# One core, one fixed set of instructions, another written-out order: new costs and priorities in a planner for linear attention and a gated MLP

## The chip, the cores and the metric

The kernel runs on one core of a Trainium2 chip. The metric is the device time of one launch in microseconds (us). The median of three runs of the kernel before is 784.33 us; they lie between 782.07 and 785.16 us.

## What is computed

The reference is linear attention with softmax-like features, followed by a block that gates, normalises and projects. Cut to what matters:

```python
def phi(x):                                   # q, k: 8 batches, 8 heads, 576 rows, 64 wide
    proj = einsum('bhsd,df->bhsf', x, w_phi)  # 128 features
    proj = proj - max(abs(proj), axis=-1)
    return concatenate([exp(proj), exp(-proj)], axis=-1)
kv, z = einsum('bhsf,bhsd->bhfd', phi(k), v), sum(phi(k), axis=2)
x = einsum('bhsf,bhfd->bhsd', phi(q), kv) / (einsum('bhsf,bhf->bhs', phi(q), z) + 1e-6)
x = x.transpose(0, 2, 1, 3).reshape(4608, 512)
h = x @ w_in                                  # 512 -> 1024
solu = h * exp(h - max(h)) / (sum(exp(h - max(h))) + 1e-9)
out = (layer_norm(solu) * g_ln) @ w_out       # 1024 -> 512
```

## The kernel before

**The attention half** works in 16 units of four heads (unit u is half of the heads of batch u // 2), and each unit in two halves of two heads ("sub" 0 and 1). For the keys, five tiles of rows are loaded (`rawk`), split into a rounded part and a rest (`xh`, `xl`; not in the first three units), projected on TensorE (`pjk`), reduced and shifted on VectorE (`m`, `dk`) and exponentiated on ScalarE (`ek`). `visit` (L651) then does all the small matmuls of a half: the sums over rows (`kvT`) and, from the seventh half on, in one stretch with it the numerators and denominators of the half before (`num`, `den`). The result is turned on VectorE (`kvs`), written to DRAM (`dk`) and read back in four pieces (`kvf`, L719).

For the queries, each half from unit 3 on loads one block of 128 x 1152 numbers, 576 KB, the "q rows" (`q_load`, L783, tile `rawq`). ScalarE rounds it (`q_hi`, L787, a cast to `hq`), GpSimd forms the rest in place (`q_lo`, L791), TensorE projects (`pq`), VectorE turns it and takes a maximum, and after a small chain over TensorE, GpSimd and ScalarE the features `fq` are made on ScalarE. The denominators go through VectorE (`den_recip`, L893: `dE`, `cmp`, `cmr`), to DRAM (`den_rows`, L903) and come back copied to 64 partitions each (`den_bcast`, L907, tile `rb`, two transfers per half). GpSimd multiplies (`xa`, `xb`).

**The second half** works on 36 tiles of 128 tokens. For each: split of x (`mxh`, `mxl`), 24 matmuls for h, maximum on VectorE (`moe_max`, L1149, `nm`), exponential on ScalarE (`moe_exp`, L1153, `eu`), product on VectorE (`eu` again), statistics (`bst`, `mv`), eight transposes (`uT`), a split into `uh` (ScalarE) and `ul` (VectorE), 24 matmuls for the output (`o`), scaling on ScalarE (`os`) and a store.

**The order.** Work of both halves is interleaved, and no scheduler runs on the chip: each engine executes its instructions in the program's order (L345 hands each instruction on with the order kept, which is why the profile shows that one line for nearly all). The order is worked out once, while the program is built, by `Plan.order` (L212). It is a list planner: each operation has an engine, a cost in nanoseconds, predecessors and tiles. At each step each engine looks at the operations that could go next. The one that could start first on it by the plan's clock is taken (TensorE may wait a little to keep its array's tiling); the priority, BASE[group] + OFFSET[kind] (L197), decides only among those that could start at that same moment. Groups are the 16 units, the 36 token tiles and the weights (53 numbers), kinds the operations within them (688 numbers). Buffers are handed out in the order of the priorities too.

A transfer has two costs, the time that it holds the issuing queue (SP, the only queue used) and the time on the DMA engines. Its landing, and what follows from it, are planned so:

```python
hold, transfer = o["cost"]
engine_free[e] = t + hold
dma_free = done[i] = max(t + hold + 625, dma_free) + transfer   # L301
# a successor may start 910 after done (1150 on TensorE), L163
```

The costs that the change touches are `dma()` at L139 for plain blocks, and figures of their own for the four pieces of `kvf` (L1019), the q rows (L1042), and the broadcasts `rb` (L1109). `den_recip` has its cost at L1105. The exponential's cost and predecessor are at L1234, the cast's at L1043.

Of the kernel before, what the change touches and what calls it, by code (L numbers as in the profile page):

```python
# [22 lines left out]
HC = S // 2  # L23
# [36 lines left out]


BASE = (
# [4 lines left out]
)  # L67
OFFSET = (
# [47 lines left out]
)  # L116


# [4 lines left out]
def dve(n):  # L123
    return (n + 65) / 0.96
# [12 lines left out]


def dma(nbytes, spread=False):  # L139
    return (580 if spread else 440), max(nbytes / 360.0, 50)  # L140


class Plan:
# [213 lines left out]
def linear_attention_then_moe(ctx: ExitStack, tc, qT, qT2, kT, v, w_phi, w_in, g_ln, w_out, out):  # L357
# [181 lines left out]
    for i in range(8):  # L539
        z, R, T = w_time[i], ("raw", i), ("w32", i)  # L540
# [406 lines left out]
    for u in range(2 * B):  # L947
# [6 lines left out]
        def add(name, engine, cost, t, fn, args, after=(), alloc=(), tiles=(), early=None):  # L954
            name = (u, *name)
            q = lambda names: [x[1] if x[0] == "abs" else (u, *x) for x in names]
            op(name, engine, cost, z0 + t * step, fn, (st, *args), q(after),
               [(tag, x[1] if x[0] == "abs" else (u, *x)) for tag, x in alloc], q(tiles), early)

        for g, (c0, n) in enumerate(TILES):  # L960
            nt, n2 = n // P, 2 * n
            z = 2.0 * g
# [28 lines left out]
        for sub in range(2):  # L991
# [23 lines left out]
            if u not in KV_PE:  # L1015
                add(("kve", sub), "vector", dve(384) + 40, z, kv_turn, (sub,), [prev], [("d", ("kvs", sub))], [("kv", sub)])
                add(("kvo", sub), "sync", dma(P * 384 * 4), z, kv_out, (sub,), [("kve", sub)], (), [("kvs", sub)])
                for i in range(4):
                    add(("kvi", sub, i), "sync", (620, 137), z, kv_in, (sub, i),  # L1019
                        [("kvi", sub, i - 1) if i else ("kvo", sub)], () if i else [("kf", ("kf", sub))], [("kf", sub)])  # L1020
            else:
                add(("kve", sub), "scalar", act(384, True), z, kv_ev, (sub,), [prev], [("d", ("kvs", sub))],
# [16 lines left out]
        for sub in range(2):  # L1039
            z = 5.0 * sub + 1.0  # L1040
            if qsp:
                add(("ql", sub), "sync", (400, 1640), z - 4, q_load, (sub,), (), [("q4", ("rq", sub))])  # L1042
                add(("qh", sub), "scalar", act(2 * S), z - 2.5, q_hi, (sub,), [("ql", sub)], [("q4", ("hq", sub))],  # L1043
                    [("rq", sub)])
                add(("qlo", sub), "gpsimd", pool(2 * S) + 130, z - 2.2, q_lo, (sub,), [("qh", sub)], (),
# [56 lines left out]
                add(("qv", sub, c), "scalar", act(HC, True), z + 5.1 + c, q_oe, (sub, c),  # L1102
                    [source["num"]] + ([("qv", sub, 0)] if c else []), () if c else [("E", ("E", sub))],
                    [("num", sub, c), ("E", sub)])
            add(("dc", sub), "vector", dve(HC) + 27 + 330, z + 6.3, den_recip, (sub,), [source["den"]],  # L1105
                [("dE", ("dE", sub))], [("den", sub)])
            add(("ds", sub), "sync", (380, 100), z + 6.5, den_rows, (sub,), [("dc", sub)])
            for j in range(2):
                add(("db", sub, j), "sync", (560, 600), z + 6.9, den_bcast, (sub, j),  # L1109
                    [("ds", sub)] + ([("db", sub, 0)] if j else [("db", 0, 1)] if sub else []), () if j else [("rb", ("rb", sub))],  # L1110
                    [("rb", sub)])
            pair = 2 * qd + sub
# [188 lines left out]
```

## Time and profile before

| | us |
|---|---|
| median of three runs | 784.33 |
| the profiled execution | 785.97 |
| its span, first to last instruction | 783.9 |
| TensorE busy (PE) | 754.0 |
| VectorE busy (DVE) | 500.1 |
| GpSimd busy (POOL) | 471.1 |
| ScalarE busy (ACT) | 384.5 |

The mean granted clock of TensorE over the span is 0.986 of full speed. A table by windows has one row per stretch: its bounds and length, then for each engine the busy time and in brackets the number of instructions, then the granted clock, the busy share of the DMA engines and GB/s. A line of the timeline has the start, the length, engine, instruction, tiles (written <- read), count, and in square brackets the idle time of that engine just before it with what ended it. PE's matmuls are pipelined, so its busy time is a cover of the time axis and not a sum of work; where PE is "busy" at half clock it does half the work.

### The profile page before, as it was taken

The page shows a single profiled execution, that of the slowest core. Times are in us where ns is not written, and L with a number is a line of the kernel's source. Part 1 is how long each engine was busy: PE and PEld are TensorE (multiplying, and loading weights), DVE is VectorE, ACT ScalarE, POOL GpSimd, SP SyncE. Part 2 cuts the span into 40 slices and gives each one's busy share as a digit, 9 for nine tenths or more (in the row PEclk, how much of TensorE's full clock was granted, in tenths as well). Part 3 has the DMA queues.
Part 4 walks back from the last instruction along what each step waited for, and adds up shares of the span by engine and source line. Part 5 has one row for each costly group of instructions (what it writes and reads, how often), then busy time and mean ns, then how long its engine had stood idle before and what let it go on. Part 6 is the DMA issues. An engine that isn't in the chain of part 4 may idle for free.

```text
span 783.9 us, 13479 instructions
## 1 busy us (share of the span) xinstructions
PE 754.0 (96%) x4935; PEld 566.1 (72%) x4935; DVE 500.1 (64%) x861; ACT 384.5 (49%) x750; POOL 471.1 (60%) x507
## 2 busy tenths in 40 slices
PE   5899999999999999989999999999999999999997
PEld 3566677767777777767776777777778776778885
DVE  3897986665775676756777657765457665444343
ACT  3757765363736445544636463633546454223221
POOL 1144788686977658676767786855677775132110
PEclk8899999999999999989999999999999999999999
DMA  7843532243415152433424342414241222110001
GB/s 233 313 148 103 138 88 84 69 144 77 129 50 158 53 141 79 117 89 102 114 57 135 95 148 62 127 56 136 77 129 44 56 56 58 42 43 13 28 15 40
DMA packets 99969, 75.35 MB, mean 96 GB/s; under 512 B 56128, under 2 KB 90432, under 8 KB 99392
## 3 DMA queue, kind: packets, MB, share of 16 engines
q1 hardware_dynamic: 99904, 74.50, 32.6%
q8 instruction: 39, 0.64, 0.3%
q14 instruction: 26, 0.21, 0.1%
HBM read 59.38 MB, written 15.09 MB: 95 GB/s over the span
## 4 chain that ended last, share of the span: by engine, by line
PE 55%; DVE 3%; DMA 2%; SPq 1%; ACT 1%; POOL 1%; issue 0%; ACTq 0%; POOLq 0%
PE o L345 18%; PE h L345 17%; PE kvT L345 5%; PE num L345 5%; PE uT L345 3%; PE pjk L345 2%; PE den L345 2%; PE pq L345 2%; DMA rawq<-in_q 2%; SPq L345 1%; DVE bst L345 0%; DVE eu L345 0%; DMA rb<-d 0%; DVE cmp L345 0%; DVE ul L345 0%
## 5 line engine op out<-in xcount | busy, mean ns | idle before, releaser
L345 ACT ACTIVATE ek<-dk 128x512 f32<-128x512 f32 (+1 forms) x160 | 88.2, 582 | 61.3 <-DVE dk L345 55.7
L345 PE MATMUL o<-w_out_h,uh 128*128 128x512 f32 x288 | 115.7, 402 | 1.2 <-DVE ul L345 1.1
L345 PE MATMUL o<-w_out_l,uh 128*128 128x512 f32 x288 | 114.1, 396 | 0.0
L345 PE MATMUL o<-w_out_h,ul 128*128 128x512 f32 x288 | 114.1, 396 | 0.0
L345 POOL TENSOR_TENSOR zacc<-zacc,ek 128x512 f32<-128x512 f32 (+1 forms) x78 | 100.8, 1292 | 18.6 <-ACT ek L345 15.2
L345 PE MATMUL h<-win_h,mxh 128*128 128x512 f32 x288 | 94.1, 408 | 0.0
L345 PE MATMUL h<-win_l,mxh 128*128 128x512 f32 x288 | 91.3, 398 | 0.0
L345 PE MATMUL h<-win_h,mxl 128*128 128x512 f32 x288 | 91.1, 397 | 0.0
L345 DVE TENSOR_TENSOR ul<-uT,uh 128x512 fp32r<-128x512 f32 x72 | 48.7, 683 | 49.2 <-ACT uh L345 49.0
L345 POOL TENSOR_TENSOR hq<-rawq,hq 64x1152 fp32r<-64x1152 f32 x26 | 69.1, 2659 | 16.6 <-ACT hq L345 14.9
L345 DVE TENSOR_REDUCE nm<-h 128x1 f32<-128x1024 f32 x36 | 44.0, 1222 | 52.6 <-PE h L345 52.5
L345 ACT ACTIVATE fq<-pT 128x576 f32<-128x576 f32 x104 | 68.5, 676 | 16.4 <-PE den L345 6.7
L345 POOL TENSOR_TENSOR blk<-blk,mcol 128x1152 f32<-128x1152 f32 x26 | 55.5, 2135 | 26.2 <-ACT mcol L345 20.6
L345 ACT CAST uh<-uT 128x512 fp32r<-128x512 f32 x72 | 41.5, 583 | 57.6 <-PE uT L345 39.0
L345 PE MATMUL num<-fq,kvf 128*64 128x288 f32 x512 | 69.2, 412 | 0.6 <-DMA kvf<-dk 0.6
L345 ACT ACTIVATE eu<-h,nm 128x1024 f32<-128x1024 f32 x36 | 40.2, 1117 | 59.5 <-DVE nm L345 59.1
L345 DVE TENSOR_TENSOR eu<-h,eu 128x1024 f32<-128x1024 f32 x36 | 44.0, 1223 | 36.5 <-ACT eu L345 36.5
L345 DVE TENSOR_REDUCE m<-pjk 128x4 f32<-128x512 f32 (+1 forms) x80 | 48.7, 623 | 24.9 <-PE pjk L345 24.5
L345 PEld LDWEIGHTS h<-win_l,mxh 128*128 128x128 f32 x288 | 54.7, 190 | 13.3
L345 PEld LDWEIGHTS h<-win_h,mxl 128*128 128x128 f32 x288 | 54.6, 190 | 13.2
L345 PEld LDWEIGHTS o<-w_out_h,uh 128*128 128x128 f32 x288 | 54.2, 188 | 13.8 <-DVE ul L345 1.9
L345 PE MATMUL kvT<-ek,rawv 128*64 128x256 f32 x512 | 64.0, 382 | 0.0
(107 smaller groups left out, 1571.7 us busy)
## 6 DMA issues: line engine op xcount, KB each, us to landing
rawq<-in_q SPq DMA_DIRECT2D x26, 576.0 KB, 5.1
rb<-d SPq DMA_DIRECT2D x64, 144.0 KB, 3.3
out<-os SPq DMA_DIRECT2D x36, 256.0 KB, 2.0
rawk<-in_k SPq DMA_DIRECT2D x64, 128.0 KB, 2.7
rawv<-in_v SPq DMA_DIRECT2D x64, 128.0 KB, 2.3
dk<-kvs SPq DMA_DIRECT2D x28, 192.0 KB, 1.9
kvf<-dk SPq DMA_DIRECT2D x112, 48.0 KB, 2.5
wraw<-in_w_in SPq DMA_DIRECT2D x4, 1024.0 KB, 6.0
```

Of the source, the lines that this page charges most:

```text
L345: return self.tc.keep_in_program_order(method(*args, **kwargs))
```

## The change

No operation is added, removed or resized: the same operations with the same predecessors, tiles and buffers go through the same planner. Changed are five lines of costs and the 741 priorities. A plain transfer is reckoned at 300 instead of 360 bytes per nanosecond; the q rows at 440 + 2600 instead of 400 + 1640 ns; each broadcast at 640 + 950 instead of 560 + 600; each piece of `kvf` at 660 + 160 instead of 620 + 137; `den_recip`'s three VectorE instructions at 880 ns together instead of dve(288) + 357 = 724.7.

```diff
 def dma(nbytes, spread=False):
-    return (580 if spread else 440), max(nbytes / 360.0, 50)
+    return (580 if spread else 440), max(nbytes / 300.0, 50)
...
-                    add(("kvi", sub, i), "sync", (620, 137), z, kv_in, (sub, i),
+                    add(("kvi", sub, i), "sync", (660, 160), z, kv_in, (sub, i),
...
-                add(("ql", sub), "sync", (400, 1640), z - 4, q_load, (sub,), (), [("q4", ("rq", sub))])
+                add(("ql", sub), "sync", (440, 2600), z - 4, q_load, (sub,), (), [("q4", ("rq", sub))])
...
-            add(("dc", sub), "vector", dve(HC) + 27 + 330, z + 6.3, den_recip, (sub,), [source["den"]],
+            add(("dc", sub), "vector", 880, z + 6.3, den_recip, (sub,), [source["den"]],
...
-                add(("db", sub, j), "sync", (560, 600), z + 6.9, den_bcast, (sub, j),
+                add(("db", sub, j), "sync", (640, 950), z + 6.9, den_bcast, (sub, j),
```

The priorities are new numbers near the old ones. The first lines of BASE (weights, then units 0 to 13) as an example:

```diff
-    -335.3, -1579.6, -520.2, 46.7, 148.7, 211.0, 261.8, 299.0, 351.4, 396.6, 438.6, 480.4, 527.0, 577.2, 625.0,
+    -420.3, -1654.0, -538.8, 32.5, 142.5, 205.1, 253.3, 303.4, 345.0, 393.4, 437.9, 482.8, 527.3, 576.3, 639.9,
```

OFFSET changes in the same manner. Counted from 0, its numbers 604 and 605 belong to the load and the cast of the q rows of sub 0 from unit 4 on, 635 and 636 to those of sub 1: they go from -34.3, -33.3, -36.0 and -19.9 to -29.8, -16.8, -36.5 and -15.8.

100 rows, old and new, of tables (BASE, OFFSET) are left out of this document.

## The prediction

> **What bounds the kernel now.** First the page, for the span and the busiest engine:
>
> ```profile
> span 783.9 us, 13479 instructions
> PE 754.0 (96%) x4935; PEld 566.1 (72%) x4935; DVE 500.1 (64%) x861; ACT 384.5 (49%) x750; POOL 471.1 (60%) x507
> ```
>
> TensorE (PE) is busy for 754.0 of 783.9 us. No instruction is removed, so a new order can only win back the remaining 29.9 us and what half clock costs. The table by windows, cut at the places where PE was idle, says where they are:
>
> ```profile
> core 0: us, PE busy (x) PEld busy (x) DVE busy (x) ACT busy (x) POOL busy (x), PEclk, DMA share, GB/s
> 0.00:10.00 10.00, 4.70 (x12) 3.20 (x12) 3.48 (x7) 3.33 (x6) 2.27 (x17) 1.00 0.59 176
> 10.00:20.00 10.00, 5.65 (x12) 3.43 (x13) 4.18 (x9) 3.27 (x6) 0.00 (x0) 0.59 0.94 297
> 20.00:30.00 10.00, 8.50 (x82) 5.53 (x80) 9.34 (x9) 6.80 (x11) 2.36 (x1) 0.90 1.04 410
> 30.00:40.00 10.00, 8.45 (x50) 5.41 (x50) 8.62 (x13) 8.60 (x16) 1.39 (x1) 0.83 0.63 223
> 40.00:110.00 70.00, 65.30 (x624) 45.74 (x616) 61.69 (x91) 46.67 (x104) 43.00 (x28) 1.00 0.42 116
> 110.00:170.00 60.00, 59.53 (x401) 44.35 (x402) 41.06 (x79) 29.61 (x61) 47.04 (x51) 1.00 0.32 97
> 170.00:178.00 8.00, 6.26 (x36) 4.69 (x34) 4.56 (x9) 6.58 (x14) 7.61 (x10) 1.00 0.50 115
> 178.00:285.00 107.00, 106.62 (x705) 80.37 (x706) 69.02 (x128) 50.83 (x99) 74.15 (x76) 1.00 0.35 96
> 285.00:290.00 5.00, 4.18 (x23) 3.44 (x22) 3.72 (x10) 4.86 (x11) 4.51 (x7) 1.00 0.40 111
> ...
> 338.00:342.86 4.86, 2.71 (x35) 1.73 (x27) 3.36 (x6) 3.76 (x7) 4.72 (x3) 1.00 0.04 14
> 342.86:349.69 6.83, 6.11 (x18) 4.98 (x19) 5.10 (x9) 3.72 (x9) 5.82 (x10) 0.50 0.40 87
> 349.69:426.00 76.31, 76.31 (x526) 57.43 (x524) 50.99 (x94) 39.32 (x78) 56.02 (x54) 1.00 0.36 104
> 426.00:434.00 8.00, 6.79 (x38) 5.56 (x37) 7.27 (x15) 5.04 (x11) 7.44 (x11) 1.00 0.50 125
> 434.00:770.00 336.00, 335.92 (x2032) 257.99 (x2031) 193.11 (x332) 144.84 (x276) 179.83 (x211) 1.00 0.24 69
> 770.00:784.00 14.00, 8.98 (x41) 6.64 (x39) 3.07 (x6) 2.44 (x4) 0.75 (x2) 0.97 0.10 37
> ```
>
> From 434 to 770 us PE is idle for 0.08 of 336 us at full clock: nothing to win, much to lose. The last 14 us (5.02 idle) are the drain of the last token tile, a chain that no order shortens much. The first 40 us lose 5.30 + 4.35 + 1.50 + 1.55 = 12.70 us of idle time plus some half clock to first loads and the preparation of weights. Between 40 and 434 us lie 4.70 (40 to 110), 0.47, 1.74, 0.38, 0.82, then 2.15, 0.72 and 1.21 us. Behind the 2.15 the clock was 0.50 for 6.83 us, in which 6.11 busy us did the work of about 3.05. So the two stretches 338 to 350 and 426 to 434 cost 2.15 + 0.72 + 3.05 + 1.21 = **7.1 us**, nearly half of all that the middle can give.
>
> What these two stretches waited for is in the chain of waits. Both times it passes through a transfer of q rows, two of its longest pieces:
>
> ```profile
> 329.08 7.68 DMA rawq<-in_q
> ...
> 413.02 6.07 DMA rawq<-in_q
> ```
>
> The timeline shows how a late transfer reached TensorE. First stretch:
>
> ```profile
> 328.61 0.85 SPq L345 DMA_DIRECT2D rawq<-in_q  x2
> ...
> 333.70 1.23 DVE L345 TENSOR_REDUCE nm<-h 128x1 f32<-128x1024 f32 x1 [1.11 <-PE h L345]
> ...
> 336.84 1.15 ACT L345 CAST hq<-rawq 128x1152 fp32r<-128x1152 f32 x1 [4.89 <-DMA rawq<-in_q]
> ...
> 338.19 1.12 ACT L345 ACTIVATE eu<-h,nm 128x1024 f32<-128x1024 f32 x1
> ...
> 339.43 1.23 DVE L345 TENSOR_TENSOR eu<-h,eu 128x1024 f32<-128x1024 f32 x1 [4.50 <-ACT eu L345]
> ...
> 340.71 0.66 PE L345 MATMUL uT<-ident,eu 128*128 128x128 f32 x4 [1.47 <-DVE eu L345]
> ...
> 343.08 0.58 PE L345 MATMUL pjk<-wph_h,xh 128*128 128x256 f32 x1 [0.91 <-DVE dE L345]
> ...
> 345.23 0.58 PE L345 MATMUL pq<-hq,w_hh 128*128 128x288 f32 x1 [0.49 <-POOL sa L345]
> ```
>
> ScalarE (ACT) keeps program order. It stood 4.89 us before the cast of the q rows, though the exponential `eu` queued behind it had its maximum at 333.70 + 1.23 = 334.93. `eu` ran at 338.19; VectorE waited 4.50 us for it, and behind VectorE's product stood everything that frees TensorE's banks. Second stretch, same shape:
>
> ```profile
> 412.39 1.01 SPq L345 DMA_DIRECT2D rawq<-in_q  x2
> ...
> 416.52 1.22 DVE L345 TENSOR_REDUCE nm<-h 128x1 f32<-128x1024 f32 x1 [0.23 <-PE h L345]
> ...
> 419.17 1.16 ACT L345 CAST hq<-rawq 128x1152 fp32r<-128x1152 f32 x1 [2.22 <-DMA rawq<-in_q]
> ...
> 421.33 1.10 ACT L345 ACTIVATE eu<-h,nm 128x1024 f32<-128x1024 f32 x1
> ...
> 427.79 0.37 PE L345 MATMUL pq<-hq,w_hh 128*128 128x288 f32 x1 [0.60 <-POOL sa L345]
> ...
> 428.90 0.50 PE L345 MATMUL o<-w_out_h,uh 128*128 128x512 f32 x1 [0.60 <-DVE ul L345]
> ```
>
> **The change, part by part.** *The q rows.* Issues and landings (KB each, median us to landing):
>
> ```profile
> rawq<-in_q SPq DMA_DIRECT2D x26, 576.0 KB, 5.1
> rb<-d SPq DMA_DIRECT2D x64, 144.0 KB, 3.3
> ...
> rawk<-in_k SPq DMA_DIRECT2D x64, 128.0 KB, 2.7
> ```
>
> The cast began 0.08 us after the landing (336.84 against 329.08 + 7.68), so a landing of the trace compares with the plan's "usable" time, landing plus 910 ns. For a single block of q rows the plan said 400 + 625 + 1640 + 910 = 3.58 us after the issue; it will say 440 + 625 + 2600 + 910 = 4.58, with 5.1 the median here. For two issued back to back, as at both places, the second was usable 3.58 + 1.64 = 5.22 us after the first issue and will be 4.58 + 2.60 = 7.18. Put on the trace's clock: at 328.61 + 5.22 = 333.83 the old plan saw the cast start before the exponential (maximum at 334.93), so it put the cast first. The new plan has 335.79, after 334.93: exponential first. At the second place it is 417.61 before, the maximum at 416.52 + 1.22 = 417.74, and 419.57 after: the order flips again, and 419.57 is past the real 419.17. The real start at the first place, 336.84, is 1.05 us later than the new figure, so ACT may still stand a little there, but with the exponential done. With the exponential at about 335 instead of 338.19, some 3 us earlier, the 1.47 us wait of `uT` and its followers go, and with them the half clock. Late next is the q chain itself (`hq`, `pq`), whose cast comes no later than now plus one exponential, 1.12 us. Value: **-7.1 us**; bounds 0 (the places come out alike) and -7.1.
>
> On the price of a q row there is a rule that speaks against the change. The Trainium skill, DMA: Bandwidth & Descriptors, Specifications, gives a core some 358 GB/s from memory and 0.6 us to the first byte; worked out from it, an estimate of 2.25 us for 576 KB, the old plan's figure and not the new one's, by which this term would be 0. The median of 5.1 us above disagrees.
>
> *Broadcasts, `kvf`, plain blocks, the reciprocal.* Usable times go from 560 + 625 + 600 + 910 = 2.70 to 3.13 us for `rb` (median 3.3), and from 2.34 to 2.41 for a 128 KB block (440 + 625 + 910 + 131072 / 360 or / 300; median 2.7). Both come nearer to the trace. What waits for `rb` is GpSimd:
>
> ```profile
> POOL xa L345 <- DMA rb<-d: 27.6, 13, 6.5
> SPq L345 <- ACT os L345: 166.7, 26, 14.6
> ```
>
> These 27.6 us are hidden: the page has POOL busy for 60%, and a later `xa` holds up PE only through the token tiles, of which PE has stock (0.08 us idle in the 336 above). Value 0; cover gone, one `rb` wait costs up to 6.5 us. The longer holds (40 ns for each of 8 pieces and 2 q rows, 80 for each of 4 broadcasts, 0.72 us per unit) exist in the plan only; the chip's SP queue stands idle anyway, 166.7 us before stores alone.
>
> *Everything else is dealt anew.* 741 priorities change, so small stalls of other causes vanish and come. None of it is visible in the trace before. The lower bound is that all idle time of 40 to 770 us goes: 4.70 + 0.47 + 1.74 + 0.38 + 0.82 + 2.15 + 0.72 + 1.21 + 0.08 = 12.3, with the half clock 15.3 us. The upper is fresh stalls of the dear kind: 2.15 + 0.72 + 3.05 = 5.9 us each. I take the plain cheap kind, once: the three places at full clock that stand alone are 1.74, 0.82 and 1.21, mean 1.26, so **+1.3 us**, since the old middle has three such in 394 us and priorities near the old ones will keep most of them as they were, so one more is already a third more. The start and the drain I take at 0; PE's first work waits for first loads.
>
> **Sum.** -7.1 + 1.3 = -5.8. The profiled execution took 785.97 us (span 783.9), 1.64 over the median of 784.33. On its own time the sum gives 780.2; on the median **778.5 us**, -0.74%. A difference under 0.5% (3.9 us) can't be told from none here, so "faster" begins below 780.4 and "slower" above 788.3.
>
> **The rivals.**
>
> *Repaid (784.4).* The two stalls go, but the new order makes one cold stall of 5.9 and one plain: -7.1 + 5.9 + 1.3. For it: 394 us of the old middle hold eight idle rows, so stalls come easily. Against: 336 us without any, under the old, shorter costs. The same time follows if the pairs of q rows are ordered as before.
>
> *Slower (789.0): the read-back is late.* Transfers thought longer are issued earlier. SP keeps order: a load put early stands before its buffer is free, and the four pieces of `kvf`, without which a visit's numerators can't start, queue behind it. A visit is at the head of TensorE's queue, so PE stops. It decides when the pieces come over about 2 us late: 1.74 us idle left the clock at 1.00, 2.15 was followed by 0.50. Two such visits cost 11.8: -7.1 + 11.8 = +4.7. For it: SP does wait much (166.7 us before stores). Against: every cost moves towards the measured landing, which makes the plan start consumers later and not loads tighter.
>
> *More than that (772.3).* The two singles 1.74 and 0.82 and half of the 4.70 in 40 to 110 us go as well, with no fresh one: -7.1 - 2.56 - 2.35 = -12.0.
>
> *No clock to win (781.6).* The half clock at 342.86 has a cause other than the idle time before it, and comes back: then the two places give only their idle 4.08, and -4.08 + 1.3 = -2.8. The row speaks against it: the drop follows the 2.15 us at once. The Trainium skill, TensorE: Matmul & The Clock Gate, Why this matters for your kernels, asks for no PE gaps over about 3 us, one idle window bringing half clock; the longest single wait of PE quoted here is 1.47 us, so by that rule the gaps would not have done it. The trace shows several short gaps in one such stretch and the clock at 0.50 behind them.
>
> **How the numbers follow.** Chances: forecast 0.46, more than that 0.13, repaid 0.20, no clock 0.06, slower 0.15. The forecast's own range is 775 to 781.5: no fresh stall and a small one gone, or three fresh ones. About 0.38 of its 0.46 lie below 780.4; with 0.13 and a hundredth of the repaid case that is 0.52 faster. Slower has its 0.15 and 0.02 of the repaid case, 0.17; 0.31 remains for the same. The range 770 to 789 reaches from the lower bound (784.33 - 15.3 = 769.0) with a corner left out to the slower case.
>
> **What would show it.** Right: near the old places, or wherever a pair of q rows is issued, the cast no longer stands more than about 2 us before an exponential that is ready; the granted clock holds 1.00 from 40 us to the drain; PE idle between 110 and 434 us falls from 7.5 us to about 2 to 4; the stretch to 770 stays dense. The landings themselves must stay at 4 to 8 us: if they shrink, the gain came from traffic and not from order. Wrong: a second stretch with clock 0.50 after 40 us; waits of `num` for `kvf` of over 2 us; more idle time before 110 us; or the exponential still queued behind a late cast.

## The result, and the profile after

| | before | after |
|---|---|---|
| median, us | 784.48 (4 runs, 782.07 to 785.16) | 774.28 (4 runs, 772.5 to 775.5) |
| ratio | | 0.9868, 95% interval 0.9842 to 0.9893 |
| profiled execution, us | 785.97 | 773.6 |
| its span, us | 783.9 | 771.7 |
| mean granted clock | 0.986 | 0.993 |

The change is 10.2 us faster, where the prediction had 5.8. The head of the page of the changed kernel:

```profile
span 771.7 us, 13472 instructions
PE 747.6 (97%) x4935; PEld 564.6 (73%) x4935; DVE 498.0 (65%) x861; ACT 384.1 (50%) x750; POOL 471.0 (61%) x507
```

The same 4935 matmuls, with 24.1 us of idle PE instead of 29.9. Where, the table by windows says (columns as in the prediction):

```profile
0.00:40.00 40.00, 27.22 (x156) 16.90 (x156) 27.49 (x39) 22.57 (x39) 7.32 (x20) 0.87 0.78 268
40.00:110.00 70.00, 65.51 (x614) 46.63 (x614) 57.71 (x89) 47.34 (x108) 44.24 (x31) 1.00 0.44 122
110.00:434.00 324.00, 322.38 (x2191) 244.35 (x2190) 220.88 (x408) 169.74 (x334) 245.76 (x252) 1.00 0.37 103
434.00:758.00 324.00, 324.00 (x1942) 250.46 (x1941) 189.29 (x325) 141.98 (x269) 172.94 (x205) 1.00 0.24 68
```

Idle time of the first 40 us is 12.78 us (12.70 before), of 40 to 110 us 4.49 (4.70). From 110 to 434 us it fell from 7.49 to 1.62 us, and the half clock there (3.05 us of work lost) is gone. Those two make 5.87 + 3.05 = 8.9 us. The clock can't be put down to the change, though. A second profile of the kernel before (span 781.5 us, its rows are further down) has the stretch at 1.00, with 7.89 us idle, and the first 40 us at 0.91, where the first profile has 0.83 and the changed kernel 0.87. Against that second profile the change is worth 6.3 us in the stretch, all of it idle time. Of the 9.8 us between those two spans 7.2 us are less idle time of PE (31.3 and 24.1 us); the other 2.6 us lie inside what the page counts as busy (750.2 and 747.6 us), where no view shows them apart.

The casts of the q rows on ScalarE, as the groups of lines have them, first in the kernel before, then in the changed one (count | busy, mean ns | idle before them and what ended it):

```profile
L345 ACT CAST hq<-rawq 128x1152 fp32r<-128x1152 f32 x26 | 30.0, 1154 | 31.8 <-DMA rawq<-in_q 15.4 <-POOL hq L345 12.3 <-DVE pT L345 2.1
```

```profile
L345 ACT CAST hq<-rawq 128x1152 fp32r<-128x1152 f32 x26 | 29.9, 1151 | 11.9 <-POOL hq L345 9.4 <-PE pq L345 1.6 <-DMA rawq<-in_q 0.8
```

ScalarE's standing for q rows went from 15.4 to 0.8 us. The rows also land sooner:

```profile
rawq<-in_q SPq DMA_DIRECT2D x26, 576.0 KB, 4.3
```

4.3 us instead of 5.1. The prediction had said that a gain with shorter landings came from traffic and not from order, so this is a rival. At the two places themselves (sub 0 of units 9 and 11, found by counting loads and casts in the program's order) the difference is larger than in the median:

```profile
317.09 0.54 SPq L345 DMA_DIRECT2D rawq<-in_q  x1
...
322.92 0.33 SPq L345 DMA_DIRECT2D rawq<-in_q  x1
...
325.92 1.12 ACT L345 ACTIVATE eu<-h,nm 128x1024 f32<-128x1024 f32 x1 [1.99 <-PE o L345]
...
327.59 1.15 ACT L345 CAST hq<-rawq 128x1152 fp32r<-128x1152 f32 x1
...
400.28 0.53 SPq L345 DMA_DIRECT2D rawq<-in_q  x1
...
405.93 0.33 SPq L345 DMA_DIRECT2D rawq<-in_q  x1
...
410.67 1.15 ACT L345 CAST hq<-rawq 128x1152 fp32r<-128x1152 f32 x1
```

The two blocks of a unit, issued 0.5 and 0.6 us apart before, are now issued 5.8 and 5.7 us apart. The later one lands 3.8 and 3.5 us after its issue instead of 7.7 and 6.1, and its cast follows an exponential without a wait. From issue to cast it is 4.7 us at both places, where it was 7.8 and 6.2: the use has not moved away from the issue, the rows land faster.

The largest idle place left between 110 and 758 us is another one, a wait of `pq` of the timeline that no transfer ended:

```profile
244.78 0.37 PE L345 MATMUL pq<-hq,w_hh 128*128 128x288 f32 x1 [1.52 <-DVE mt L345]
```

### The profile page after: what moved, and what is told of

Same layout as the page of the kernel before. It is cut to its first block, busy times and chain, and to the rows that moved or that the text cites. A ratio compares the mean times of both kernels' runs of the same rounds, so it can differ in the third digit from the quotient of the medians.

```text
span 771.7 us, 13472 instructions
## 1 busy us (share of the span) xinstructions
PE 747.6 (97%) x4935; PEld 564.6 (73%) x4935; DVE 498.0 (65%) x861; ACT 384.1 (50%) x750; POOL 471.0 (61%) x507
## 4 chain that ended last, share of the span: by engine, by line
PE 93%; DVE 3%; DMA 1%; ACT 1%; SPq 1%; issue 1%; POOL 0%; ACTq 0%; POOLq 0%
PE o L345 26%; PE h L345 26%; PE kvT L345 11%; PE num L345 8%; PE pjk L345 6%; PE uT L345 4%; PE den L345 4%; PE pq L345 4%; DVE w L345 1%; PE pjq L345 1%; PE dT L345 1%; SPq L345 1%; DMA rawk<-in_k 1%; DVE cmp L345 0%; DVE m L345 0%
## 5 line engine op out<-in xcount | busy, mean ns | idle before, releaser
L345 POOL TENSOR_TENSOR blk<-blk,mcol 128x1152 f32<-128x1152 f32 x26 | 55.5, 2135 | 36.5 <-ACT mcol L345 36.3
L345 PEld LDWEIGHTS o<-w_out_h,ul 128*128 128x128 f32 x288 | 54.2, 188 | 13.2
```

The source lines that it names most:

```text
L345: return self.tc.keep_in_program_order(method(*args, **kwargs))
```

## The experiments

Three theories went in. **A**, the prediction's: late q rows at two places, by standing in front of a ready exponential, cost 7.1 us. **B**: all transfers were planned too short, the planner's clock ran too fast everywhere, and places are only where this surfaces. **C**: costs do not matter; the priorities, or the traffic, do. To weigh B a number of the kernel's own is used: the clock on which `Plan.order` lays out the order. Its end is 766.5 us for the order before and 770.0 for the changed one. It can also be added up over a finished order with other costs: the order before, with the new costs, ends at 782.7. These figures are arithmetic of the kernel's code and no measurement; what is measured is how the spans stand to them.

### The two casts behind the exponentials

```diff
-    for o in plan.order():
+    sequence = plan.order()
+    for first, then in (((9, "qh", 0), ("moe", 10, "ex")), ((11, "qh", 0), ("moe", 13, "ex"))):
+        sequence = behind(sequence, first, then)   # `first` and what hangs on it go behind `then`
+    for o in sequence:
```

> The kernel before with its order kept, except at the two places of the prediction: the cast of the q rows (unit 9 and unit 11, sub 0) and the GpSimd subtraction that hangs on it are put behind the exponential that waited behind the cast (token tiles 10 and 13). Theory A (the prediction's: a late block of q rows in front of a ready exponential cost these two places 7.1 us): about 777 us, -7 against before, clock 1.00 from 40 us on, no idle time of TensorE over 0.5 us at either place. Theory B (the places only show where a plan that is too fast everywhere runs out of slack; freed here, the delay comes up at the next place): within 2 us of before. Theory C (the rows land sooner in the changed kernel because they are issued apart): no change, since the issues are as before.

783.85 us against 784.9, ratio 0.9983 (0.9962 to 1.0003): at most 3 us, and not told from nothing. The windows of its profile around the two places:

```profile
338.00:350.00 12.00, 10.40 (x55) 8.28 (x54) 8.13 (x16) 6.42 (x12) 11.59 (x16) 1.00 0.39 93
350.00:426.00 76.00, 74.57 (x516) 55.69 (x515) 52.70 (x98) 41.87 (x82) 56.41 (x58) 1.00 0.37 106
```

And the timeline, at the first place (three lines) and the second:

```profile
333.21 1.12 ACT L345 ACTIVATE eu<-h,nm 128x1024 f32<-128x1024 f32 x1
334.71 1.15 ACT L345 CAST hq<-rawq 128x1152 fp32r<-128x1152 f32 x1 [0.29 <-DMA rawq<-in_q]
...
344.55 0.37 PE L345 MATMUL pq<-hq,w_hh 128*128 128x288 f32 x1 [0.87 <-DVE dk L345]
...
420.77 0.29 PE L345 MATMUL mtp<-ident,m 128*36 128x128 f32 x1 [1.01 <-ACT E L345]
```

The flip did locally what it should: the exponential runs at once, ScalarE waits 0.29 us instead of 4.89, no wait of `uT` is left, and the clock stays at 1.00 (as it does without the flip in the second profile of the kernel before, so the flip isn't shown to have saved it). But 1.60 us of idle time stays at the first place, now before `pq`, the projection of the same late rows; and at the second a wait of 1.01 us stands before the matmul behind it, for a copy `E` that ScalarE does after the cast of the unit's other block. Between the casts and these waits stand GpSimd's rests of the q rows, one at a time, and VectorE waits for them too:

```profile
335.99 2.65 POOL L345 TENSOR_TENSOR hq<-rawq,hq 64x1152 fp32r<-64x1152 f32 x1 [4.03 <-ACT hq L345]
...
342.62 0.48 DVE L345 STREAM_TRANSPOSE blk<-pq 128x288 f32<-128x288 f32 x1 [2.47 <-POOL hq L345]
...
419.26 1.15 ACT L345 CAST hq<-rawq 128x1152 fp32r<-128x1152 f32 x1 [2.51 <-POOL hq L345]
```

The rows land as late as before (7.5 and 6.1 us after their issue, against 7.7 and 6.1), and PE's own order still asks for what is made of them.

### The q rows earlier

All blocks of sub 0 first, then only the two of the two places: a buffer of their own, issued some 4 us earlier. The diff is that of the two; for all, the condition takes every load of sub 0.

```diff
-    for o in plan.order():
+    LEAD, sequence, own = 4000.0, plan.order(), {}
+    for o in [o for o in sequence if o["name"] in ((9, "ql", 0), (11, "ql", 0))]:
+        own[o["name"]] = 0                           # a buffer "rq" of its own
+        i = sequence.index(o)
+        while plan.start[sequence[i - 1]["name"]] > plan.start[o["name"]] - LEAD:
+            i -= 1
+        sequence.remove(o)
+        sequence.insert(i, o)
+    for o in sequence:
```

> The kernel before with its order kept, except that each block of q rows of sub 0 from unit 3 on has a buffer of its own and is issued some 4 us earlier on SP. Theory A: the casts find their rows landed, the waits of ScalarE for q rows (15.4 us in all before) fall under 5, and the two places give back their 7 us: 777. Theory B: the casts no longer wait, but the other transfers are as late against the plan as before, so about half: 780 to 782. Theory C: the rows land sooner than the median of 5.1 us since the pairs are pulled apart, and the time falls with it, to 777.

786.63 against 784.9, ratio 1.0019 (1.0002 to 1.0037): a little slower, where every theory had a gain. ScalarE waited for no block of q rows any more (15.4 us before), as A had it, and the time did not follow. The two windows of its profile with half clock after 40 us:

```profile
40.00:60.00 20.00, 15.94 (x147) 10.89 (x147) 14.22 (x19) 11.36 (x24) 6.85 (x4) 0.91 0.34 102
130.00:142.00 12.00, 10.12 (x75) 7.40 (x72) 7.81 (x13) 7.76 (x14) 9.51 (x11) 0.86 0.27 78
```

4.06 and 1.88 us of idle time with a clock of 0.91 and 0.86; the kernel before had 2.54 us idle in the first, 0.47 in all of 110 to 170 us, and full clock in both. In the first, PE waited 3.4 us for an early unit's q rows of 128 KB, where the kernel before had 0.4:

```profile
PE pjq L346 <- DMA rawq<-in_q: 3.4, 1, 3.4
```

So at least there, moving loads ahead on one queue delayed another. In the second window the longest wait is 1.9 us of `pq` for VectorE, and its link to the queue isn't shown. So only the two:

> The kernel before with its order kept, except that the two blocks of q rows of the two places alone (units 9 and 11, sub 0) have a buffer of their own and are issued some 4 us earlier on SP. Theory A: both places lose their idle time and clock, 777 to 778. Theory B: both places lose their idle time, but what they cost in most executions is less than in the profile, 781 to 783. A rival to both (the order of SP is so tight that any load moved ahead delays another): 784 or more, as when all blocks were moved.

779.56 against 784.56, ratio 0.9931 (0.9904 to 0.9958): -5.4 us, between 3.3 and 7.5. The window that held the first place:

```profile
338.00:350.00 12.00, 12.00 (x67) 9.74 (x67) 8.61 (x16) 5.74 (x12) 10.83 (x17) 1.00 0.37 93
```

No idle time, full clock. The time lies between what A (777 to 778) and B (781 to 783) expected. The two blocks were issued 4.5 and 3.2 us ahead of the unit's other block and landed 4.7 and 4.5 us after their issue. Late rows at these two places cost about 5 us, then, and what cures it is rows that have landed, not ScalarE's order. Two things changed at once here, the earlier issue and the distance between the two loads, and no run of this order has one without the other.

### The kernel before once more

> The kernel before once more, for a second profile. If the half clock at 342 us belongs to the order, it is there again, with 2 us of idle time ahead of it and 4 to 5 us of waiting before the cast of unit 9. If it belongs to one execution, the place shows idle time of under 2 us and clock 1.00, and theory A's price of 7.1 us was read from an unlucky run.

783.6 us, span 781.5. The same two windows as in the prediction, and three long ones:

```profile
338.00:342.86 4.86, 2.39 (x21) 2.01 (x17) 4.32 (x7) 3.76 (x9) 4.84 (x3) 1.00 0.06 22
342.86:349.69 6.83, 5.64 (x29) 4.67 (x28) 5.92 (x12) 3.16 (x7) 6.04 (x11) 1.00 0.45 108
...
0.00:40.00 40.00, 27.49 (x174) 17.51 (x176) 28.06 (x42) 22.31 (x38) 7.00 (x19) 0.91 0.84 289
40.00:110.00 70.00, 64.30 (x602) 44.51 (x599) 64.30 (x87) 47.74 (x107) 42.79 (x29) 1.00 0.40 109
110.00:434.00 324.00, 316.11 (x2106) 237.93 (x2106) 218.48 (x398) 168.16 (x329) 242.96 (x250) 1.00 0.36 101
```

The wait is there again (2.47 and 1.19 us idle, 3.7 in all), the half clock is not. Neither outcome that was named came as a whole: the idle time belongs to the order, the half clock to one execution. So the first place costs 3.7 or 5.9 us by execution, and 7.1 for both was read from the dearer one.

### Costs and priorities, one without the other

The five cost lines of the change with the priorities of before, and the reverse.

> The five cost lines of the change with the priorities of before. The planner's own clock, worked out while the order is made, ends at 796.3 us for this order (766.5 for before, 770.0 for the changed kernel). Theory B (the new costs make that clock true): the span is 3 us or less from 796.3. Theory A: much the same, with q rows the only term that matters, so up to 5 us over it. Theory C (priorities or traffic, costs do not matter): near before, 780 to 788.

801.48 us, ratio 1.0205 (1.0189 to 1.0222); span 800.0, 3.7 over the clock. B had asked for 3 or less, A for up to 5.

> The priorities of the change with the costs of before. The planner's own clock ends at 814.7 us with the old costs; the same order added up with the new costs ends at 821.1. Theory B: the span is within 4 us of 821 and so 6 or more over the plan's own clock. Theory A: about 815 to 819. Theory C (the new priorities are simply better or sturdier): near the changed kernel, 770 to 780.

824.09 us, ratio 1.0477 (1.0426 to 1.0529); span 824.5. Each half alone is slower than either kernel: a priority has a meaning only against the costs it was found with. "Priorities alone" of theory C is out by 44 us. The spans stand 3.7 and 3.4 us over what the new costs add up to, so these costs tell the chip's time to a few us over a range of 50 us.

These two orders also show which half pulled the pairs of q rows apart. With the new costs and the old priorities the blocks of units 9 and 11 are still issued 0.5 and 0.6 us apart and the later ones land after 6.2 and 5.6 us; with the new priorities and the old costs it is 9.5 and 5.7 us apart, and 4.1 and 3.3 us. So it is the new priorities that pull them apart, with either costs.

### Late rows on purpose

Ahead of each of the 26 blocks of q rows, in both kernels, a transfer that nothing reads:

```diff
 def q_load(st, sub):
+    other = dram.tile([64, 2 * S], F32, tag="other", name="other")
+    nc.sync.dma_start(out=other, in_=qT[st["b"], 2 * st["qd"] + sub, :64].rearrange("d a s -> d (a s)"))
     st["rq", sub] = sb("q4", [P, 2, S], name="rawq")
```

> The kernel before with one added transfer of 288 KB between two places in DRAM, which nothing reads, ahead of each of the 26 blocks of q rows; so those land later, by an estimated 1 to 1.5 us. Theory B, sturdiness part (the changed order has room for late transfers where the order before has none): 10 to 25 us slower than without the transfers. Rival (both orders are equally sensitive, the change only shifted the start): the same increase as in the changed kernel.

> The changed kernel with the same added transfers ahead of the 26 blocks of q rows. Theory B, sturdiness part: 3 to 10 us slower than the changed kernel (774.28), under half of the increase of the kernel before. Rival: the same increase as there.

Before: 794.72 us, ratio 1.0138 (1.0105 to 1.017), some 10 to 11 us more. The changed kernel: 772.66, ratio 0.9843 to before (0.9807 to 0.988): no more than the 774.28 without the transfers. ScalarE's waits for q rows (us in all, times, longest), first in the kernel before with the transfers, then in the changed one:

```profile
ACT hq L345 <- DMA rawq<-in_q: 30.1, 10, 6.8
```

```profile
ACT hq L345 <- DMA rawq<-in_q: 7.6, 8, 2.2
```

The added transfers made the rows land 0.8 and 1.0 us later (medians 5.9 and 5.3 us). In the order before, ScalarE's wait doubles from 15.4 to 30.1 us. The changed order takes rows that land later in the median (5.3) than those of the kernel before did (5.1) without losing time, where 3 to 10 us were expected. So the shorter median is not what makes it faster. The two places are another matter: with the added transfers, too, the two loads of a unit are issued 5.2 and 5.0 us apart there, and the later blocks still land after 4.8 and 3.6 us, not 7.7 and 6.1. For them the traffic half of theory C (rows that land sooner because they are issued apart) is not out; it fits the flip, which left the landings and gained little, and the two loads moved, which shortened them and gained 5.4 us.

### The same search with either costs

Priorities searched anew, each time about 490,000 orders, looking at the planner's clock alone and starting from the other kernel's priorities; then the one with new costs went on with random lateness of all transfers in what it looked at. The diffs are the numbers of BASE and OFFSET alone.

> The five cost lines of the change; priorities from a search of our own, some 490,000 orders, which started from the priorities of before (796.3 us on the planner's clock with these costs) and looked at that clock alone: no random lateness, no replays. It ends at 765.3. Theory B (true costs are what made the change faster): the span is 1 to 4 us over that clock, 766.5 to 769.5, so the time is about 769 to 772, faster than before by some 13 and not behind the changed kernel. Theory L (a rival: without tuning on late transfers an order is brittle, and that tuning made the change faster): 5 us or more over the clock, time 773 to 785.

773.98 us, ratio 0.9856 (0.9812 to 0.9901), span 772.7.

> The control to the kernel searched with the new costs: the costs of before, the same search with as many orders, started from the priorities of the change (814.7 us with these costs). It ends at 763.2 on the planner's clock; the same order added up with the new costs ends at 775.3. Theory B: the span is 1 to 4 us over 775.3 and 13 or more over its own clock, so the time is 778 to 782, some 8 to 12 slower than the other search. Rival (more search is all there is to it, whatever the costs): span within 4 of 763, level with the other search or ahead.

777.62 us, ratio 0.9923 (0.9892 to 0.9953), span 776.2.

> The new costs; the search of search_new_costs went on from where it ended with 540,000 more orders, and now looked at 0.3 times the planner's clock plus 0.7 times the mean of six additions of the order in which every transfer lands later by a random time (exponential, mean 0.15 us plus 0.35 of its transfer time). The planner's clock ends at 765.0. Theory B: 1 to 3 us over that clock, time 768 to 771, within 2 us of search_new_costs. Theory L: faster than search_new_costs by 3 us or more. Either way it should beat both kernels.

772.83 us, ratio 0.984 (0.9795 to 0.9885), span 769.3. It is the fastest order here, but its interval overlaps with the changed kernel's, so it isn't shown to beat it. All orders together (us; the first two columns are the planner's arithmetic):

| order | own costs | new costs | span of the profile | over new costs | spans of all runs (median) |
|---|---|---|---|---|---|
| before | 766.5 | 782.7 | 783.9, 781.5 | 1.2, -1.2 | 777.9 to 786.6 (782.8) |
| after | 770.0 | 770.0 | 771.7 | 1.7 | 770.6 to 773.6 (772.4) |
| new costs, priorities of before | 796.3 | 796.3 | 800.0 | 3.7 | 799.1 to 800.2 (799.7) |
| costs of before, new priorities | 814.7 | 821.1 | 824.5 | 3.4 | 815.0 to 824.5 (822.3) |
| searched with costs of before | 763.2 | 775.3 | 776.2 | 0.9 | 774.0 to 778.3 (775.8) |
| searched with new costs | 765.3 | 765.3 | 772.7 | 7.4 | 770.9 to 772.7 (772.2) |
| and then with lateness | 765.0 | 765.0 | 769.3 | 4.3 | 769.3 to 771.3 (770.9) |

The orders made with the old costs run 10 to 17 us over their own clock; added up with the new costs, they are within 3.4. Theory B holds in this: the old clock was too fast, and by it the order before (766.5) was better than the changed one adds up to. Two larger expectations of it missed. The search with new costs should have been within 4 of its clock and was 7.4 over (6.9 by the median span), which is what rival L had said; and its lead over the control is 3.6 us and not 8 to 12. L missed in its turn: looking at lateness was to bring 3 us or more and took back 3 of the 7.4 in the profiled spans, 1.2 us in the medians, which these runs don't tell from nothing. That a search which looks at the clock alone uses up the room that late transfers need would explain the 7.4 us; no run shows it.

The runs of the two searches do not overlap, so the order found with true costs is faster by some 4 us. But there is one search with either costs, each from another start, and how far two searches with the same costs differ was not measured; that true costs are worth 4 us is therefore likely and not shown. How the change's own 10 us divide between costs, lateness and how long it was searched, stays open.

## Why the prediction came out as it did

**Where the gain could lie: right.** Nothing came from 434 to 758 us, and the start and the drain kept their idle time; the 110 to 434 us stretch gave 8.9 us against the profile that the prediction read and 6.3 against the second one. The prediction expected 2 to 4 us of idle time there and a clock of 1.00: it is 1.62, and 1.00. The time itself, 774.28, lies in the wide range but below the forecast's own 775 to 781.5: its two terms erred in opposite ways, the one too large and the other with the wrong sign, and partly cancelled.

**The term of the q rows, -7.1: right in kind, large by about a third.** Late rows at the two places cost 5.4 us (3.3 to 7.5), by the run that issued just these two blocks earlier. The size came from one profile whose half clock the second one doesn't have.

**The step that failed** is in the same part: "With the exponential at about 335 instead of 338.19, some 3 us earlier, the 1.47 us wait of `uT` and its followers go, and with them the half clock." The waits went, and the time did not: 1.05 us by the medians, -0.2 to 3.0 by the interval. The prediction took the queue of ScalarE for the cause and said that late next would be the q chain, without a price. It had one: `pq` stands at a fixed place in PE's order, and the numerators' copy `E` behind the cast in ScalarE's. In the changed order the casts do stand behind an exponential, as forecast (another tile's). What the prediction did not have is that the pairs of loads come apart: it worked out both places with two blocks back to back. They are issued over 5 us apart now and land after 3.8 and 3.5 us instead of 7.7 and 6.1. By its own sign (landings under 4 us mean traffic and not order) the gain at these two places came with shorter landings, by an order that issues the loads apart.

**The fresh stall, +1.3: the mis-sized term.** One came (1.52 us before `pq` at 244.78), as forecast. But I let the other cheap places stand, and they went: 110 to 170 us gave back 0.47, 170 to 178 us 1.74, 285 to 290 us 0.82. If the rows gave the 5.4 us that they gave in the run with two loads moved, all the rest is -4.8 us instead of +1.3. The value 0 for plain blocks and broadcasts went by whether their own waits hurt PE today. Added up on the planner's clock with one new cost at a time, the order before ends 5.7 us later by the plain blocks, 3.1 by the q rows, 2.5 by the broadcasts, 1.1 by the reciprocal and 0.1 by `kvf`; with all of them together it is 16.2. That is arithmetic, and no run gave the costs one by one, but by it the plain blocks weigh more than the q rows on which the prediction staked its sum, and small delays add up to more together than one by one.

**The rivals.** "Repaid" and "slower" did not occur: the changed kernel's profile has no cold stall after 40 us. `num` waited nowhere on a read-back in the changed kernel. "More than that", 772.3, was the nearest, and by its mechanism: the singles of 1.74 and 0.82 went as well, though the 4.70 us of 40 to 110 us did not halve (4.49). "No clock to win" leaned on the row where the drop follows the idle time; the repeat shows that like idle time needn't bring it.

## What to carry to other kernels

An order written out against a clock that is too fast for transfers hides its loss: each late transfer looks like a small stall of its own. Before moving instructions, set the planner's figure for each kind of transfer against the trace's time from issue to landing, back-to-back issues included, and add up the present order with the true ones. Here moving one consumer behind another cured little while the rest of the late chain kept its place; loads issued earlier and apart from each other did. Before putting down a gain to the order of the consumers, look at when the data landed at the very place that improved: the median over all loads (5.1 and 4.3 us) hid what the two places show (7.7 and 3.8).

## What the runs showed of the hardware

A block of 576 KB took 5.1 us from issue to landing in the median of the kernel before, and two issued 0.5 us apart (at 328.61 and 329.08 us) took 6.8 and 7.7. In the five units of that kernel whose two blocks were issued within 0.7 us, the second landed after 6.1 to 7.7 us; blocks with no other such load within 2 us of them took 3.4 to 5.4. Half clock has no plain threshold in idle time: 2.15 us idle in 4.86 us was followed by 0.50 for 6.83 us, 2.47 us idle before the same matmuls of another execution by none. In the kernel before with added transfers, one idle stretch was long enough by itself:

```profile
345.40:349.50 4.10, 0.68 (x11) 0.28 (x3) 1.52 (x2) 3.02 (x6) 2.86 (x2) 1.00 0.02 5
349.50:352.91 3.41, 3.41 (x17) 3.07 (x15) 3.34 (x6) 3.41 (x6) 3.39 (x2) 0.50 0.21 63
```

3.42 us idle, then 0.50 for 3.41 us. The Trainium skill (TensorE: Matmul & The Clock Gate, Why this matters for your kernels) names gaps of over about 3 us; this row (3.42 us) agrees, and the row with 2.15 us shows that several shorter ones were followed by half clock too, in one execution of two.
